# Attention and two gated layers in one kernel: four units normalized behind the value product, and a new order

## The chip, the cores and the metric

The kernel runs on one core of a Trainium2 chip. The metric is the device time of one execution in microseconds (us). The five engines are TensorE (PE; its weight loads are PEld), VectorE (DVE), ScalarE (ACT), GpSimd (POOL) and SyncE (SP), which issues the DMAs.

## The reference

Block-causal attention over 4 batches of 8 heads, 576 positions and 64 dimensions, then two feed-forward layers of 512 to 2048 to 512, in 32-bit floats.

```python
scores = scale * np.matmul(q, k.transpose(0, 1, 3, 2))
scores = np.where(mask, scores, -1000000000.0)     # mask: block of 64 of i >= that of j
scores = scores - np.max(scores, axis=-1, keepdims=True)
attn = np.exp(scores)
attn = attn / (np.sum(attn, axis=-1, keepdims=True) + 1e-09)
x = (attn @ v), heads side by side: 2304 tokens x 512
h = x @ w_in;  g = 1 where h >= 1, 0 where h <= -1, else (h + 1) ** 2 / 4;  x = g @ w_out
h = x @ w_in2; g = max(0.01 * h, h);                                       out = g @ w_out2
```

## The kernel before, in words

The attention is cut into 32 units: a pair of heads (the 128 partitions of a transposed result) and a part of the queries, "a" (the first 320 positions, three chunks of 64, 128 and 128 rows) or "b" (the last 256, two chunks). `unit_scores` multiplies queries by keys into PSUM slots of two banks (L586; L590 where the operands are split in two rounded parts) and calls `softmax`: per chunk a masked block is set (L482), the row maximum is taken on DVE (L484), ACT takes the exponential of every head and chunk into SBUF and sums its rows (L491), ACT adds 1e-9 (L495), DVE takes the reciprocal (L497), and POOL multiplies every probability by it (L502). Before that POOL clears the columns between the last key of a chunk and the next multiple of 128 (L606), and scales the queries (L547). `unit_values` transposes the probabilities in 128x128 blocks on PE (L680, against the identity), copies them out of PSUM on ACT or DVE (L685, L687), multiplies them by the values (L696), and evacuates the sum: for the first 256 tokens of the batch (the first four units, all of part "a") the rounded part to `XB[0]` on ACT (L707) and the rest on DVE (L708), the other columns through `xp` (L710) by DMA to DRAM (L711).

The weights of the first layer arrive as 64-bit words and are rebuilt in 16 steps (`w_float`) by ACT (L431, L442), POOL (L432, L445) and DVE (L434, L439, L445), two steps to a tile `W[p]`. `h1_block` then multiplies block i of 256 tokens by the eight tiles `W[p]`, 24 matmuls of 256 columns each into one PSUM bank (L756), which ACT and DVE evacuate (L762, L766, L767). Block 0 reads its tokens straight from `XB[0]`, all four quarters of it (one per pair of heads). The second product of the layer (L943) and both of the next (L1066, L1127) follow in a Strassen-like form with seven products.

No order is written by hand. Every operation is recorded with an engine, a cost and a priority, and `Plan.schedule` makes the order of each engine by a randomized list search with `TRIES` attempts from `SEED`; the chosen order is then issued as it is, so every engine works through its list in that order, and an instruction that waits holds up all behind it. PSUM has eight banks: slots 0, 1, 3 for attention, slot 2 as a fourth for the first seven units, and after these its two banks (4 and 5) for `h1_block`, of which block 0 uses only bank 4.

Of the kernel before, what the change touches and what calls it, by code (L numbers as in the profile page):

```python
# [25 lines left out]
SA = 320  # L26
# [23 lines left out]

AHEAD = 45.0


# [9 lines left out]

SEED, TRIES = 13, 42

# [239 lines left out]
def fused_kernel(ctx, tc, qk, qk2, v, w1, w2, out):  # L305
# [44 lines left out]
    def pool(cols, prio, fn, r, w, fixed=161):  # L350
        plan.op("POOL", fixed + 0.95 * cols, prio, fn, r, w, fixed != 200)

# [37 lines left out]
    def slot(i):  # L390

        return Bank(plan, (2 * i, 2 * i + 1), lambda: slots[i], {1: ps_b, 2: ps_c}.get(i, ps_a))

# [20 lines left out]
    def w_float(prio, fc):  # L414

        raw, sg = (C[8 + fc % 5].reg(z, m) for z, m in ((0, 1024), (1024, 512)))
        hs = XS.reg(turn("hs", (0, 512, 1024)), 512)
        src = w1[fc, :, 0:1024]  # L420
        t, j = W[fc // 2], fc % 2
        s = slice(512 * j, 512 * j + 512)

        def words():
            return raw.get().bitcast(I32).rearrange("p (n t) -> p n t", t=2)

        def upper():
# [11 lines left out]
        dve(512, prio, lambda: nc.vector.scalar_tensor_tensor(  # L439
            dst.get().bitcast(I32), hs.get().bitcast(I32), 3, sg.get().bitcast(I32),  # L440
            op0=ALU.logical_shift_left, op1=ALU.bitwise_or), [hs, sg], [dst])
        act(512, prio, lambda: nc.scalar.activation(t.get()[:, 0, s], dst.get(), AF.Copy), [dst], [(t, (j, j + 1))], sb=on_pool)  # L442

        def low():
            (nc.gpsimd if on_pool else nc.vector).tensor_tensor(t.get()[:, 1, s], dst.get(), bc(t.get()[:, 0, s]), op=ALU.subtract)  # L445
        rw = [dst, (t, (j, j + 1))], [(t, (2 + j, 3 + j))]
        if on_pool:
            plan.op("POOL", 1225, prio, low, *rw, True)
        else:
            dve(512, prio, low, *rw)  # L450

# [11 lines left out]
    dve(0, -100, lambda: nc.vector.memset(wz.get(), 0.0), [], [wz], fixed=200)  # L463
    zp = slot(2)
    for i in range(N_WARM):
        pe(427, -1000, lambda: nc.tensor.matmul(zp.get()[:, 0, 0:128], lhsT=wz.get(), rhs=wz.get(), start=True, stop=True), [wz], [zp])

# [3 lines left out]

    def softmax(prio, tag, s, parts):


        n = sum(len(p[2]) for p in parts)
        nm, sm, rs = small("nm", f"nm{tag}"), small("sm", f"sm{tag}"), small("rs", f"rs{tag}")
        i = 0
# [10 lines left out]
        for c, _, heads, view, probs, pbufs in parts:  # L488
            keys = CH[c][2]
            for k in range(len(heads)):  # L490
# [25 lines left out]
    def unit_scores(pair, part, prio, ring, room_):  # L516
# [16 lines left out]
        qk_room = qs, qo, nqk  # L533
        units[pair, part] = vt, pr, prob

# [64 lines left out]
        for c in ((0, 1, 2) if part == "a" else (3, 4)):  # L600
            keys = CH[c][2]
            a, b_ = PCOL[c] + keys, PCOL[c] + (keys + 127) // 128 * 128
            for hd in range(2):
                if a == b_:
                    continue
                pool(0, prio - 1, lambda a=a, b_=b_, hd=hd: nc.gpsimd.memset(prob(hd, a, b_), 0.0), [], [part_of(hd, a, b_)], fixed=200)  # L606

# [7 lines left out]
        for grp in groups:  # L615
            s = slot(ring[0])
            ring.append(ring.pop(0))

            def f(grp=grp, s=s):
                for i, (c, o) in enumerate(grp):  # L620
                    for hd in range(2):
                        score(s.get()[:, hd, o:o + CH[c][2]], c, hd, 0, CH[c][2], i == 0)
            pe(score_cost(sum(CH[c][2] for c, _ in grp)), prio, f, ready, [s])
            softmax(prio, f"{n}_{grp[0][0]}", s, [
                (c, o, (0, 1), lambda s=s, o=o, c=c: s.get()[:, :, o:o + CH[c][2]],
                 [probs(c, 0), probs(c, 1)], [pbuf(c, 0), pbuf(c, 1)]) for c, o in grp])
        if part == "b":
# [10 lines left out]
            for hd in range(2):  # L638
                if ss:
                    s = ss[hd]  # L640
                else:
                    s = slot(ring[0])

                    def f(hd=hd, s=s):
# [4 lines left out]
                    (4, 224, (hd,), lambda s=s: flat2(s)[:, 224:800].rearrange("p (h k) -> p h k", h=1),  # L649
                     [probs(4, hd)], [pbuf(4, hd)])])  # L650

# [10 lines left out]
    def unit_values(pair, part, prio, ring, evac):  # L662
        n = f"{part}{pair}"
        vt, pr, prob = units[pair, part]
        pts = []
        for i, blocks in enumerate(TILES[part]):
# [23 lines left out]
        ring.append(ring.pop(0))  # L690
        nq = SA if part == "a" else SB

        def f():
# [5 lines left out]
        pe(sum(x[3] for x in SUMS[part]) * 1.7 + 150, prio, f, [vt] + pts, [s])  # L699
        xp = P2.reg(turn("xp", (4032, 4352)), SA)  # L700
        b, kc = divmod(pair, NKC)
        c0 = b * S + (0 if part == "a" else SA)

        q0 = 256 if c0 == 0 else 0
        if q0:
            x = XB[0]
# [37 lines left out]
    def h1_block(i, p0, dp, hbanks):  # L744

        xt = XB[i]
        for p in range(NP2):
            pr = p0 + 2 * dp * p
            ps = bank(hbanks[0])
            hbanks.append(hbanks.pop(0))  # L750
            for j in range(2):
                fc = 2 * p + j
# [440 lines left out]
    for i in range(NBLK):  # L1193
# [108 lines left out]
```

## Time and profile before

| | |
|---|---|
| median of 3 runs | 947.88 us (946.68 to 949.87) |
| the profiled execution | 946.55 us |
| its span on the chip | 944.8 us |
| TensorE busy | 924.5 us, 98% of the span |
| DVE, ACT, POOL busy | 759.3, 537.9, 321.2 us |

How to read it: the span is from the first to the last instruction, and the execution is 1.75 us longer. Engines work side by side, each through its own list. "Busy" counts the time in which an engine works on an instruction; for TensorE that is close to a bound, since its matmuls follow each other without a gap wherever nothing is late. In a table by stretch, numbers in brackets count instructions (an fp32 matmul counts twice) and PEclk is the clock granted to TensorE as a share of 2.4 GHz. "A <- B" in a list of waits reads: A waited for B.

### The profile page before, as it was taken

To read this page: it belongs to the slowest core of one execution; us is meant where nothing else is said; L and a number is where in the kernel's file an instruction comes from. 1 tells how busy PE (TensorE), PEld (TensorE's weight loads), DVE (VectorE), ACT (ScalarE), POOL (GpSimd) and SP (SyncE) were. 2 spreads that over 40 slices of the span, in tenths; PEclk is the share of its full clock that TensorE was granted. 3 is DMA by queue.
4 is the path that set the end of the run, shared out by engine and by line. 5 is a ranking of instruction groups with operands and counts; after the bars stand their busy time and mean duration, and the time that the engine had idled before them with its cause. 6 is when DMAs were issued, how large, how long until landed. Compare 5 with 4: busy or idle time off the path is not lost.

```text
span 944.8 us, 19895 instructions
## 1 busy us (share of the span) xinstructions
PE 924.5 (98%) x7324; PEld 876.0 (93%) x7324; DVE 759.3 (80%) x1289; ACT 537.9 (57%) x1060; POOL 321.2 (34%) x626
## 2 busy tenths in 40 slices
PE   7799999999999999999999999999999999999998
PEld 5467888888889999999999999999999999999998
DVE  4988867877889765779979697678888899887967
ACT  5888777877879666663334343344535563333422
POOL 6997767677665831000000020236653000000000
PEclk8999999999999999999999999999999999999999
DMA  8767878895879789976434599978885983453433
GB/s 278 235 197 224 269 255 284 297 303 185 277 264 325 262 313 326 332 246 206 149 104 143 155 348 326 342 251 276 298 292 195 322 263 91 156 156 102 145 90 113
DMA packets 168130, 221.91 MB, mean 235 GB/s; under 512 B 10080, under 2 KB 141664, under 8 KB 168032
## 3 DMA queue, kind: packets, MB, share of 16 engines
q1 hardware_dynamic: 168032, 220.63, 72.0%
q8 instruction: 58, 0.95, 0.4%
q14 instruction: 40, 0.33, 0.1%
HBM read 139.85 MB, written 80.74 MB: 233 GB/s over the span
## 4 chain that ended last, share of the span: by engine, by line
PE 91%; DVE 3%; issue 1%; ACT 1%; DMA 1%; POOL 1%; SPq 0%; DVEq 0%; ACTq 0%
PE bank L1127 30%; PE bank L756 22%; PE bank L943 18%; PE bank L1066 6%; PE slot L680 5%; PE slot L696 5%; PE slot L586 2%; PE slot L590 2%; DMA w<-w 1%; ACT rp L491 1%; DVE ra L851 1%; POOL rp L502 1%; DVE ra L1086 0%; DVE rp L687 0%; DVE wraw L1115 0%
## 5 line engine op out<-in xcount | busy, mean ns | idle before, releaser
L756 PE MATMUL bank<-ra,w 128*128 128x256 f32 x1728 | 229.2, 286 | 1.0 <-DVE rg L767 1.0
L756 PEld LDWEIGHTS bank<-ra,w 128*128 128x128 f32 x1728 | 213.2, 189 | 10.1 <-issue 5.6
L943 PE MATMUL bank<-rp,w 128*128 128x288 f32 x1344 | 180.9, 296 | 0.2 <-DVE rp L883 0.2
L943 PEld LDWEIGHTS bank<-rp,w 128*128 128x128 f32 x1344 | 179.5, 189 | 0.9 <-DVE rp L883 0.4
L851 DVE TENSOR_TENSOR ra<-ra,bank 128x288 f32<-128x288 f32 (+2 forms) x280 | 126.3, 488 | 39.9 <-ACT ra L853 13.2
L1127 PE MATMUL bank<-w,rp 128*128 128x256 f32 x1014 | 148.6, 281 | 0.0
L1127 PEld LDWEIGHTS bank<-w,rp 128*128 128x128 f32 x1014 | 132.8, 188 | 0.0
L1112 ACT ACTIVATE rp<-ra 128x1024 fp32r<-128x1024 f32 (+1 forms) x48 | 47.3, 988 | 75.7 <-DVE ra L1086 71.4
L811 POOL TENSOR_TENSOR w<-w 128x128 f32<-128x128 f32 x128 | 65.6, 533 | 41.9 <-DVE w L807 40.5
L1127 PE MATMUL bank<-rp,w 128*128 128x256 f32 x508 | 76.8, 282 | 0.0
L947 ACT ACTIVATE ra<-ra 128x1152 f32<-128x1152 f32 x32 | 37.4, 1168 | 68.0 <-DVE ra L851 68.0
L767 DVE SCALAR_TENSOR_TENSOR rg<-bank,rg 128x512 f32<-128x512 f32 x72 | 49.3, 685 | 28.5 <-ACT rg L766 28.2
L1127 PEld LDWEIGHTS bank<-rp,w 128*128 128x128 f32 x508 | 67.5, 188 | 0.1
L762 ACT ACTIVATE rg<-bank 128x512 f32<-128x512 f32 x72 | 43.0, 598 | 33.0 <-PE bank L756 32.5
L878 POOL TENSOR_TENSOR xs<-xs,rp 128x576 f32<-128x576 f32 x1 | 1.5, 1500 | 175.3 <-DMA xs<-x2d 175.3
L1115 DVE TENSOR_TENSOR wraw<-ra,rp 128x1024 fp32r<-128x1024 f32 (+1 forms) x48 | 54.3, 1134 | 6.9 <-PE bank L1127 2.4
L1127 PE MATMUL bank<-w,wraw 128*128 128x256 f32 x294 | 58.7, 282 | 0.2 <-DVE wraw L1115 0.2
L1086 DVE TENSOR_TENSOR ra<-rp,ra 128x256 f32<-128x256 f32 (+2 forms) x102 | 44.4, 439 | 2.3
L1127 PE MATMUL bank<-rg,w 128*128 128x256 f32 x280 | 46.3, 282 | 0.0
L766 ACT ACTIVATE rg<-rg 128x512 f32<-128x512 f32 x72 | 45.5, 632 | 1.0
L1086 DVE TENSOR_TENSOR ra<-rp 128x512 f32<-128x512 f32 (+2 forms) x51 | 34.4, 676 | 14.5 <-DMA rp<-gd 13.5
L1127 PEld LDWEIGHTS bank<-w,wraw 128*128 128x128 f32 x294 | 45.0, 188 | 0.6 <-DVE wraw L1115 0.4
(170 smaller groups left out, 1840.4 us busy)
## 6 DMA issues: line engine op xcount, KB each, us to landing
rp<-gd SPq DMA_DIRECT2D x41, 512.0 KB, 4.2
wcd<-w SPq DMA_DIRECT2D x43, 448.0 KB, 5.2
gd<-ra SPq DMA_DIRECT2D x32, 576.0 KB, 4.6
gd<-rg SPq DMA_DIRECT2D x64, 256.0 KB, 4.0
w<-wcd SPq DMA_DIRECT2D x32, 512.0 KB, 6.8
w<-wcd SPq DMA_DIRECT2D x32, 384.0 KB, 6.2
w<-w SPq DMA_DIRECT2D x44, 256.0 KB, 5.2
w<-w SPq DMA_DIRECT2D x16, 512.0 KB, 4.7
```

The lines of the kernel that those rows point to most:

```text
L680: nc.tensor.transpose(s.get()[:, hd, o:o + 128], prob(hd, a, a + 128), ident.get())
L696: nc.tensor.matmul(s.get()[64 * hd:64 * hd + 64, 0, q0:q0 + m], lhsT=vt.get()[:, j, 64 * hd:64 * hd + 64], rhs=pts[i].get()[:, hd, o:o + m ...
L756: nc.tensor.matmul(ps.get()[:, 256 - j * 256:512 - j * 256], lhsT=win(fc, c, kc), rhs=xt[x].get()[:, kc], start=(k == 0 and kc == 0 and j ...
L767: dve(512, pv, lambda ps=ps, gt=gt: nc.vector.scalar_tensor_tensor(gt.get(), ps.get(), 1.0, gt.get(), op0=ALU.max, op1=ALU.min), [ps, gt], ...
L811: plan.op("POOL", 430, prio, lambda o=o, a=a, b=b, op=op: nc.gpsimd.tensor_tensor(sl(o), sl(a), sl(b), op=op), [(fx, (a, a + 1)), (fx, (b, ...
L851: dve(cols, prio, lambda: nc.vector.tensor_tensor(out(o), out(a), P[b][1](), op=op), [P[b][0], (slots, (a, a + 1))], [(slots, (o, o + 1))])
L943: nc.tensor.matmul(ps.get()[:, 0:HALF], lhsT=wc(1, p, cw, li, 128 * kc, 128 * kc + 128), rhs=r.get()[:, cx, kc], start=(k == 0 and kc == 0 ...
L1066: nc.tensor.matmul(ps[t].get()[:, 0:n], lhsT=wc(z, p, cw, li, 128 * t, 128 * t + 128), rhs=x.get()[:, n * zi:n * zi + n], start=(p == 0 an ...
L1086: dve(cols, pv, lambda f=f: nc.vector.tensor_tensor(*f(), op=ALU.subtract), r, [(tt, w)], port=True)
L1112: act(4 * n, pv, lambda tt=tt, ht=ht: nc.scalar.activation(s_(ht, 0, 4), s_(tt, 0, 4), AF.Copy), [tt], [ht], sb=True)
L1115: dve(4 * n, pv, lambda tt=tt, ht=ht, lt=lt: nc.vector.tensor_tensor(s_(lt, 0, 4), s_(tt, 0, 4), bc(s_(ht, 0, 4)), op=ALU.subtract), [tt, ...
L1127: nc.tensor.matmul(ps.get()[:, 256 * t:256 * t + w], lhsT=b if wide else g, rhs=g if wide else b, start=(p == 0 and k == 0 and t == 0), st ...
```

## The change

For the first four units (`LATE = 4`) POOL no longer multiplies the probabilities. The reciprocals of their row sums are kept in a small tile `late`, PE spreads them over 64 partitions per head by a product with the identity into the second bank of the slot that takes the values' product, ACT copies that to `xp`, DVE multiplies the values' product by it in `xp`, and the split for block 0 is made from `xp`. For the first two tiles of block 0 (`EARLY = 2`) the matmuls go quarter by quarter of the tokens, each needing one pair of heads alone. The columns between chunks are cleared only where the room last held the other part. Slot 2 is no longer lent to attention; both its banks serve `h1_block` from block 0 on. Some costs and the seed and number of attempts of the search differ, so that the order of all engines is new.

```diff
-SEED, TRIES = 13, 42
+SEED, TRIES = 15, 260
...
-    ps_c = psum("psr", "psr", "ps_c", (), ((2, True),), "right")
-    ps_e = psum("psr", "psr", "ps_e", ("psr",), ((2, False),), "right")
+    ps_e = psum("psr", "psr", "ps_e", (), ((2, False),), "right")
...
-        dve(8, prio, lambda: nc.vector.reciprocal(rs.get()[:, 0:n], rs.get()[:, 0:n]), [rs], [rs])
+        act(n, prio, lambda: nc.scalar.activation(r(), sm.get()[:, 0:n], AF.Copy, bias=1e-9), [sm], mine, sb=True, extra=60)
+        dve(8, prio, lambda: nc.vector.reciprocal(r(), r()), mine, mine)
+        if late is not None:
+            return
...
-                if a == b_:
+                if a == b_ or padded.get(room_) == part:
                     continue
...
+        if late is not None:
+            def f():
+                for i, c in enumerate((0, 1, 2) if part == "a" else (3, 4)):
...
+                        nc.tensor.matmul(s.get()[64 * hd:64 * hd + 64, 1, q:q + r], lhsT=late.get()[0:r, 2 * i + hd:2 * i + hd + 1].to_broadcast([r, 64]),
+                                         rhs=ident.get()[0:r, 0:r], start=True, stop=True, skip_group_check=True)
+            pe(nq * 1.7 + 150, prio, f, [ident, late], [s])
+            act(nq, prio, lambda: nc.scalar.activation(xp.get()[:, 0:nq], s.get()[:, 1, 0:nq], AF.Copy), [s], [xp])
...
+        if late is not None:
+            dve(nq, prio, lambda: nc.vector.tensor_tensor(xp.get()[:, 0:nq], s.get()[:, 0, 0:nq], xp.get()[:, 0:nq], op=ALU.mult), [s, xp], [xp])
+            if q0:
+                x = XB[0]
+                act(q0, prio, lambda: nc.scalar.activation(x[0].get()[:, kc], xp.get()[:, 0:q0], AF.Copy), [xp], [(x[0], (kc, kc + 1))], sb=True)
+                dve(q0, prio, lambda: nc.vector.tensor_tensor(
+                    x[1].get()[:, kc], xp.get()[:, 0:q0], bc(x[0].get()[:, kc]), op=ALU.subtract), [xp, (x[0], (kc, kc + 1))],
+                    [(x[1], (kc, kc + 1))], port=True)
...
+            for kc in range(NKC if i == 0 and p < EARLY else 0):
+                for j in range(2):
...
+                    pe(3 * 119.5, pr - 8 * (NKC - 1 - kc) + 0.01 * j, f, [(W[p], (j, j + 1)), (W[p], (2 + j, 3 + j))]
+                       + [(x, (kc, kc + 1)) for x in xt], [ps])
...
-    ring.append(2)
     attention(seq[:7])
-    ring.remove(2)
-    hb = [4]
+    hb = [4, 5]
```

Over the whole program PE gets 24 matmuls more (16 of 128 columns, 8 of 64), POOL 24 multiplications and 124 clears less (36 stay of 160), DVE four instructions more; ACT and SP keep their counts.

The order moves in three places that matter here. First, PE behind the warm-up matmuls (`rp` holds queries, keys and probabilities, `w_1` of L586 and L601 the third unit's queries; slots are named by `slot`). Before:

```order
L586 MATMUL slot_150<-rp_1_93 128x64 x2
L586 MATMUL slot_150<-rp_1_93 128x192 x2
L586 MATMUL slot_88<-rp_1_93 128x320 x2
L586 MATMUL slot_88<-w_1_110 128x64 x2
L586 MATMUL slot_88<-w_1_110 128x192 x2
L680 MATMUL slot_131<-ident,rp_1_93 128x128 x6
L680 MATMUL slot_132<-ident,rp_1_93 128x128 x6
L586 MATMUL slot_131<-w_1_110 128x320 x2
L696 MATMUL slot_150<-rp_1_90,rp_1_93 64x320 x2
L696 MATMUL slot_150<-rp_1_90,rp_1_93 64x256 x2
L696 MATMUL slot_150<-rp_1_90,rp_1_93 64x128 x2
```

Now (L601 is the old L586, L697 the old L680, L724 the old L696, L716 the spread):

```order
L601 MATMUL slot_149<-rp_1_96 128x64 x2
L601 MATMUL slot_149<-rp_1_96 128x192 x2
L601 MATMUL slot_134<-rp_1_96 128x320 x2
L697 MATMUL slot_135<-ident,rp_1_96 128x128 x6
L697 MATMUL slot_149<-ident,rp_1_96 128x128 x6
L601 MATMUL slot_135<-w_1_116 128x64 x2
L601 MATMUL slot_135<-w_1_116 128x192 x2
L716 MATMUL slot_134<-ident,latea_204 64x64 x2
L716 MATMUL slot_134<-ident,latea_204 64x128 x4
L601 MATMUL slot_149<-w_1_116 128x320 x2
L724 MATMUL slot_134<-rp_1_91,rp_1_96 64x320 x2
L724 MATMUL slot_134<-rp_1_91,rp_1_96 64x256 x2
```

The second chunk group of the second unit now takes the slot of the first unit's first group, and the transposes stand ahead of the third unit's scores; the spread of the first unit's reciprocals has come in ahead of its values.

Second, POOL at the same point of the program, where line 502 multiplies probabilities and L432 (now L433) rebuilds weights. Before:

```order
L432 TENSOR_SCALAR w_1_139<-w_1_139 128x512
L502 TENSOR_SCALAR rp_1_93<-rp_1_93,rsa_0_177 64x64 x2
L502 TENSOR_SCALAR rp_1_93<-rp_1_93,rsa_0_177 128x192
L502 TENSOR_SCALAR rp_1_93<-rp_1_93,rsa_2_186 128x320
L502 TENSOR_SCALAR rp_1_93<-rp_1_93,rsa_0_177 128x192
L502 TENSOR_SCALAR rp_1_93<-rp_1_93,rsa_2_186 128x320
L547 TENSOR_SCALAR rp_1_93<-rp_1_93 128x320
L502 TENSOR_SCALAR rp_1_90<-rp_1_90,rsa_2_221 128x320
L502 TENSOR_SCALAR rp_1_90<-rp_1_90,rsa_0_218 64x64
L502 TENSOR_SCALAR rp_1_90<-rp_1_90,rsa_0_218 128x192
L502 TENSOR_SCALAR rp_1_90<-rp_1_90,rsa_0_218 64x64
```

Now:

```order
L562 TENSOR_SCALAR w_1_116<-w_1_116 128x320
L433 TENSOR_SCALAR w_1_128<-w_1_128 128x512
L433 TENSOR_SCALAR w_1_156<-w_1_156 128x512
L562 TENSOR_SCALAR rp_1_96<-rp_1_96 128x320
L433 TENSOR_SCALAR w_1_180<-w_1_180 128x512
L562 TENSOR_SCALAR rp_1_96<-rp_1_96 128x256
L433 TENSOR_SCALAR w_1_219<-w_1_219 128x512
L446 TENSOR_TENSOR w_1_246<-w_1_156,w_1_246 128x512
L621 MEMSET rp_1_91 128x64
L433 TENSOR_SCALAR w_1_242<-w_1_242 128x512
```

The two units' twelve multiplications are gone (and twelve more behind them), and the rebuilding of weights has moved up into their place.

Third, PE where an "a" unit is transposed (L680, L697) and the next "a" unit's scores follow (L586, L601), with the matmuls of block 0 (L756; L793 in its first two tiles now, L803 in the others) between them. At the transposes of pair 5, before:

```order
L680 MATMUL slot_131<-ident,rp_1_93 128x128 x6
L756 MATMUL bank_638<-ra_1_288,w_1_417 128x256 x12
L586 MATMUL slot_131<-rp_1_93 128x64 x2
L586 MATMUL slot_131<-rp_1_93 128x192 x2
L680 MATMUL slot_132<-ident,rp_1_93 128x128 x6
L586 MATMUL slot_132<-rp_1_93 128x320 x2
L756 MATMUL bank_638<-ra_1_288,w_1_543 128x256 x4
```

Now, for the same pair:

```order
L697 MATMUL slot_149<-ident,rp_1_96 128x128 x6
L803 MATMUL bank_89<-ra_1_299,w_1_551 128x256 x12
L601 MATMUL slot_149<-rp_1_96 128x64 x2
L601 MATMUL slot_149<-rp_1_96 128x192 x2
L697 MATMUL slot_134<-ident,rp_1_96 128x128 x6
L803 MATMUL bank_89<-ra_1_299,w_1_551 128x256 x8
L803 MATMUL bank_88<-ra_1_299,w_1_682 128x256 x8
L601 MATMUL slot_134<-rp_1_96 128x320 x2
L724 MATMUL slot_135<-rp_1_91,rp_1_96 64x320 x2
```

And now, one such unit earlier, for pair 4:

```order
L697 MATMUL slot_149<-ident,rp_1_96 128x128 x6
L793 MATMUL bank_89<-ra_1_299,w_1_407 128x256 x3
L601 MATMUL slot_149<-rp_1_96 128x64 x2
L601 MATMUL slot_149<-rp_1_96 128x192 x2
L697 MATMUL slot_134<-ident,rp_1_96 128x128 x6
L601 MATMUL slot_134<-rp_1_96 128x320 x2
L724 MATMUL slot_135<-rp_1_91,rp_1_96 64x320 x2
```

In the second piece matmuls of block 0 stand between the transposes through a slot and the 128x320 scores that take this slot next; in the first, and now at pair 4, the scores stand right behind. Block 0 alternates between two banks. Its first matmuls now stand behind the second unit's values, in pieces of three to nine; before, they stood behind the fifth unit's.

## Rows read from the trace of the kernel before

**Rows 1.** The page, parts 1 and 2: busy time; granted clock in 40 slices.
```profile
PE 924.5 (98%) x7324; PEld 876.0 (93%) x7324; DVE 759.3 (80%) x1289; ACT 537.9 (57%) x1060; POOL 321.2 (34%) x626
...
PEclk8999999999999999999999999999999999999999
```

**Rows 2.** Stretch, its length; busy PE, PEld, DVE, ACT, POOL; clock, DMA share, GB/s.
```profile
0.00:24.00 24.00, 16.95 (x110) 12.80 (x112) 11.79 (x32) 14.06 (x53) 15.78 (x60) 0.86 0.80 274
24.00:60.00 36.00, 30.44 (x232) 19.82 (x228) 33.35 (x68) 30.70 (x98) 33.32 (x62) 1.00 0.71 226
60.00:110.00 50.00, 46.44 (x371) 37.62 (x372) 43.59 (x84) 41.91 (x119) 39.16 (x84) 1.00 0.78 233
110.00:900.00 790.00, 789.63 (x6276) 765.31 (x6275) 639.65 (x1044) 438.04 (x769) 232.99 (x422) 1.00 0.74 241
900.00:944.80 44.80, 41.06 (x342) 40.49 (x340) 30.94 (x64) 13.17 (x22) 0.00 (x0) 1.00 0.34 106
```

**Rows 3.** What TensorE waited for, whole span: us, times, longest.
```profile
PE slot L586 <- ACT rp L491: 6.2, 3, 5.3
PE slot L680 <- POOL rp L502: 2.2, 3, 1.0
PE slot L586 <- DVE rp L687: 2.2, 2, 1.1
PE slot L680 <- DVE ra L708: 1.3, 3, 0.7
...
PE bank L756 <- DVE rg L767: 1.0, 1, 1.0
PE slot L586 <- POOL w L811: 0.8, 1, 0.8
```

**Rows 4.** Stretches around the fall of the clock, columns as in Rows 2.
```profile
10.00:11.00 1.00, 0.00 (x0) 0.00 (x0) 0.00 (x0) 0.44 (x1) 0.40 (x1) 1.00 0.94 349
11.00:12.00 1.00, 0.00 (x0) 0.00 (x0) 0.71 (x2) 1.00 (x6) 0.91 (x2) 0.53 1.08 408
12.00:17.00 5.00, 4.25 (x20) 3.32 (x20) 2.55 (x8) 4.48 (x21) 4.67 (x10) 0.50 1.03 416
```

**Rows 5.** Line 502 alone until 33.5 us: length, busy POOL; clock, DMA share, GB/s.
```profile
0.00:33.50 33.50, 11.61 (x24) 0.90 0.81 271
```

**Rows 6.** Line 606 alone, until 110 us, same columns.
```profile
0.00:110.00 110.00, 8.71 (x84) 0.97 0.76 240
```

**Rows 7.** Timeline of TensorE: start, us, instructions, idle before.
```profile
12.71 1.44 PE L586 MATMUL slot<-w 64*128 64x64 f32 x8 [5.29 <-ACT rp L491]
14.08 3.18 PE L680 MATMUL slot<-ident,rp 128*128 128x128 f32 x12
...
18.25 1.41 PE L696 MATMUL slot<-rp,rp 128*64 128x320 f32 x12
```

**Rows 8.** ScalarE alone, three units' exponentials: length, busy ACT; clock, DMA.
```profile
7.09:21.13 14.04, 11.88 (x50) 0.76 0.97 350
```

**Rows 9.** Lines 434 and 708, until 110 us: ns min/median/max, first and last start.
```profile
L434 DVE SCALAR_TENSOR_TENSOR w<-w x16: 661/692/1284, 11.3 to 87.8; 128x512 int32<-128x512 int32 x16
...
L708 DVE TENSOR_TENSOR ra<-slot,ra x4: 416/424/425, 20.7 to 38.3; 128x256 fp32r<-128x256 f32 x4
```

**Rows 10.** Groups by shape until 110 us: busy us, mean ns.
```profile
L434 DVE SCALAR_TENSOR_TENSOR w<-w 128x512 int32<-128x512 int32 x16 | 13.1, 826 | 2.2 <-POOL w L432 2.2
...
L431 ACT ACTIVATE xs<-w 128x512 f32<-128x512 f32 x16 | 10.9, 681 | 1.8 <-DMA w<-w 0.8 <-DVE w L445 0.8 <-issue 0.2
...
L445 DVE TENSOR_TENSOR w<-xs,w 128x512 fp32r<-128x512 f32 x8 | 5.8, 730 | 0.0
...
L442 ACT ACTIVATE w<-xs 128x512 fp32r<-128x512 f32 x8 | 5.2, 645 | 0.0
...
L710 ACT ACTIVATE rp<-slot 128x320 f32<-128x320 f32 x4 | 1.8, 454 | 0.0
...
L710 ACT ACTIVATE rp<-slot 128x64 f32<-128x64 f32 x4 | 0.9, 231 | 0.0
```

More of the change, by code (lines that the diff above doesn't have):

```diff
@@ L51 @@
 AHEAD = 45.0
+LATE = 4
+EARLY = 2
 DELAY = {
@@ L390, in slot @@
     def slot(i):
[L392 removed]
+        return Bank(plan, (2 * i, 2 * i + 1), lambda: slots[i], {1: ps_b}.get(i, ps_a))
     def bank(i):
@@ L449, in w_float @@
         else:
-            dve(512, prio, low, *rw)
+            dve(512, prio, low, *rw, port=True)
     def win(fc, c, kc):
@@ L463, in fused_kernel, with softmax @@
     dve(0, -100, lambda: nc.vector.memset(wz.get(), 0.0), [], [wz], fixed=200)
-    zp = slot(2)
+    zp = bank(4)
     for i in range(N_WARM):
-        pe(427, -1000, lambda: nc.tensor.matmul(zp.get()[:, 0, 0:128], lhsT=wz.get(), rhs=wz.get(), start=True, stop=True), [wz], [zp])
+        pe(427, -1000, lambda: nc.tensor.matmul(zp.get()[:, 0:128], lhsT=wz.get(), rhs=wz.get(), start=True, stop=True), [wz], [zp])
     dummy = Buf(plan, "dummy", 1, lambda: const.tile([128, 8], F32, name="dummy"))
     act(8, -1000, lambda: nc.scalar.activation(dummy.get(), wz.get()[:, 0:8], AF.Exp), [wz], [dummy], extra=1280)
-    def softmax(prio, tag, s, parts):
+    def softmax(prio, tag, s, parts, late=None):
         n = sum(len(p[2]) for p in parts)
-        nm, sm, rs = small("nm", f"nm{tag}"), small("sm", f"sm{tag}"), small("rs", f"rs{tag}")
+        nm, sm = small("nm", f"nm{tag}"), small("sm", f"sm{tag}")
         i = 0
@@ L533, in unit_scores @@
         qk_room = qs, qo, nqk
-        units[pair, part] = vt, pr, prob
+        late = pt(st, [128, 6], F32, "late", f"late{n}", 6) if len(units) < LATE else None
+        units[pair, part] = vt, pr, prob, late
         q0, k0, nq, nk, nj = (SA, 0, SA, SA, 3) if part == "a" else (0, SB, SB, S, 5)
@@ L625, in unit_scores @@
                 (c, o, (0, 1), lambda s=s, o=o, c=c: s.get()[:, :, o:o + CH[c][2]],
-                 [probs(c, 0), probs(c, 1)], [pbuf(c, 0), pbuf(c, 1)]) for c, o in grp])
+                 [probs(c, 0), probs(c, 1)], [pbuf(c, 0), pbuf(c, 1)]) for c, o in grp], late)
         if part == "b":
@@ L663, in unit_values @@
         n = f"{part}{pair}"
-        vt, pr, prob = units[pair, part]
+        vt, pr, prob, late = units[pair, part]
         pts = []
@@ L691, in unit_values @@
         nq = SA if part == "a" else SB
+        xp = P2.reg(turn("xp", (4032, 4352)), SA)
+        if late is not None:
+            def f():
+                for i, c in enumerate((0, 1, 2) if part == "a" else (3, 4)):
+                    r = CH[c][1]
+                    q = CH[c][0] - (0 if part == "a" else SA)
+                    for hd in range(2):
+                        nc.tensor.matmul(s.get()[64 * hd:64 * hd + 64, 1, q:q + r], lhsT=late.get()[0:r, 2 * i + hd:2 * i + hd + 1].to_broadcast([r, 64]),
+                                         rhs=ident.get()[0:r, 0:r], start=True, stop=True, skip_group_check=True)
+            pe(nq * 1.7 + 150, prio, f, [ident, late], [s])
+            act(nq, prio, lambda: nc.scalar.activation(xp.get()[:, 0:nq], s.get()[:, 1, 0:nq], AF.Copy), [s], [xp])
         def f():
@@ L698, in f @@
                                      skip_group_check=True)
-        pe(sum(x[3] for x in SUMS[part]) * 1.7 + 150, prio, f, [vt] + pts, [s])
-        xp = P2.reg(turn("xp", (4032, 4352)), SA)
+        pe(sum(x[3] for x in SUMS[part]) * 1.7 + 230, prio, f, [vt] + pts, [s])
         b, kc = divmod(pair, NKC)
@@ L704, in unit_values @@
         q0 = 256 if c0 == 0 else 0
+        if late is not None:
+            dve(nq, prio, lambda: nc.vector.tensor_tensor(xp.get()[:, 0:nq], s.get()[:, 0, 0:nq], xp.get()[:, 0:nq], op=ALU.mult), [s, xp], [xp])
[5 more added lines that the diff above has]
+                    [(x[1], (kc, kc + 1))], port=True)
+            dma(128 * (nq - q0) * 4, prio, lambda: nc.sync.dma_start(x1d[:, kc, c0 + q0:c0 + nq], xp.get()[:, q0:nq]), [xp],
+                [(f"x1d{kc}", (c0 + q0, c0 + nq))])
+            return
         if q0:
@@ L750, in h1_block, with f @@
             hbanks.append(hbanks.pop(0))
-            for j in range(2):
+            for kc in range(NKC if i == 0 and p < EARLY else 0):
+                for j in range(2):
+                    def f(fc=2 * p + j, j=j, kc=kc, ps=ps):
+                        for k, (c, x) in enumerate(((0, 0), (1, 0), (0, 1))):
+                            nc.tensor.matmul(ps.get()[:, 256 - j * 256:512 - j * 256], lhsT=win(fc, c, kc),
+                                             rhs=xt[x].get()[:, kc], start=(k == 0 and kc == 0 and j == 0),
+                                             stop=(k == 2 and kc == NKC - 1), skip_group_check=True)
+                    pe(3 * 119.5, pr - 8 * (NKC - 1 - kc) + 0.01 * j, f, [(W[p], (j, j + 1)), (W[p], (2 + j, 3 + j))]
+                       + [(x, (kc, kc + 1)) for x in xt], [ps])
+            for j in range(0 if i == 0 and p < EARLY else 2):
                 fc = 2 * p + j
```

25 lines of the change are left out of this document (16 added, 9 removed).

## The prediction

> **What bounds the kernel now.** I read the page first. TensorE is busy for 924.5 of 944.8 us [rows 1], so the time is its work plus the 20 us in which it has none, and no other engine is near that share. The second row of the page shows the granted clock: 2.4 GHz everywhere but in the first slice.
>
> Then the table by stretch, to see where the 20 us lie [rows 2]. From 110 to 900 us TensorE lacks 0.37 us of 790. The last stretch lacks 3.7 us, the tail behind the last matmul (evacuation, sums, the output's DMA), which the change does not touch. All else is at the start: 7.05 us of the first 24, 5.56 of the next 36, 3.56 of the 50 after that. So the change can win only in the first 110 us, at most some 15 us of the 16.2 (TensorE cannot begin with the span), and anything that it adds to TensorE's work behind 110 us is paid in full. The same rows show what keeps TensorE waiting: from 24 to 60 us VectorE is busy for 33.35 of 36 us, POOL for 33.32, ScalarE for 30.70. Attention and the rebuilding of weights share these three.
>
> Then TensorE's waits [rows 3]: 5.3 us at once for exponentials (slots of the third unit's scores), 2.2 for POOL's multiplications in three pieces, 2.2 for VectorE's copies of transposes (L687) in two, 1.0 for the evacuation of block 0's only bank (L767), 0.8 for POOL's L811, and small ones.
>
> Last the stretch with the clock [rows 4, 7]: the 5.29 us gap ends at 12.71, and by 11 us the clock has fallen to 1.2 GHz, where it is until 17 us at least. TensorE's 4.25 busy us from 12 to 17 would be 2.1 at full rate.
>
> **The change, part by part.**
>
> *POOL.* The 24 multiplications of the first four units go: 11.61 us, all before 33.5 us [rows 5]. Of the clears 36 of 160 stay; 84 stood before 110 us with 8.71 us [rows 6], so at least 48 of these go, 5.0 us at 0.104 us each. Together 16.6 of POOL's 88.3 busy us before 110 us [rows 2]. POOL is not the path by itself; the gain is what waited for it.
>
> *The first three units.* The first transposes, twelve records at 14.08 us [rows 7], had POOL's multiplications before them, and now follow the exponentials. But ScalarE is in step with this stretch: it works from 7.09 us to the third unit's last sum at 21.1 us [rows 8] with some 2 us of breaks. Up to that point its new list has two rebuilding steps L431 less and one L442 more (-2 x 0.681 + 0.645), and the first spread's copy of 320 columns (0.454, by L710 of that shape) in place of the first unit's two evacuations, of 64 columns (0.231) and of 256 (between these two) [rows 10]. That is 0.7 to 0.95 us less; I take **-0.8 us**. The ends are 0 (the steps are only put off) and -2.9 us (the first unit's six multiplications, a quarter of the 11.61, were all that stood in TensorE's way). The two spreads and the three-slot ring of these units lie in the same stretch, beside ScalarE's work, and cost nothing as long as ScalarE sets it; without that cover they cost 1.2 us.
>
> *The gaps from 24 to 110 us*, 9.1 us [rows 2]. The 1.0 us for L767 goes, since block 0 has two banks. Of the 2.2 us for L687 one half stays: where pair 5 is transposed, and once more behind it, TensorE waited for the copy that frees the slot, and there matmuls of block 0 stand between now; but at pair 4 the scores stand right behind the transposes, and TensorE has to wait as it did. 1.1 us stays. Of the 2.2 us for POOL's multiplications the piece of the fourth unit goes and the others shrink, since POOL has a fifth less to do: 0.9 stays. The remaining 3.7 us are small waits for ScalarE, VectorE and POOL. Into that stretch the change puts 48 matmuls of block 0 in pieces of three to nine, that need one pair of heads each and not all four, from the second unit's values on, where before the first stood behind the fifth unit's. I let them fill half: 1.9 stays. So 3.9 us stay and **-5.2 us** go. The ends are -8.0 (all but the 1.1) and 0 (each piece itself waits for weights, which VectorE, POOL and ScalarE rebuild).
>
> *The spread on TensorE*: six fp32 matmuls for each unit, 320 columns for each of two heads that lie side by side in the array. The nearest row is the values' product of the same shape, 704 columns for each of two heads in 1.41 us at full clock [rows 7], so 320/704 of that, 0.64 us. If the heads did not overlap, 1.28. Two units lie in the first stretch; the other two are added work: **+1.3 us** (ends 0 and 5.1, all four unpaired and none covered).
>
> *VectorE*: per unit a product of 320 columns from PSUM (0.424 x 320/256 = 0.53) and a subtraction of 256 columns inside SBUF (0.37, half of the 0.730 of L445 for 512) in place of 0.424 [rows 9, 10]: 0.47, in four units 1.9 us more, on an engine that is 93% busy from 24 to 60 us. Against it stands that L434, with both inputs in SBUF, takes 661 ns at the least and 1284 at the most [rows 9], a slowing that I put down to POOL; its mean over 16 (0.826) is 134 ns above its median [rows 9, 10], and POOL has a fifth less to do. I give back 1.0 us over all such instructions, and count half of the rest as felt: **+0.4 us** (ends +1.9 and -0.6). *ScalarE*: the 320-column copies add about 0.9 us in four units, 0.2 of it behind the stretch counted above, beside other work.
>
> The Trainium skill, "SBUF — State Buffer", section "SBUF: two separate sides", speaks against the change here: VectorE and GpSimd share a port pair that is held by one of them for a whole instruction, and a VectorE instruction with two SBUF inputs is among those that take it. The old subtraction read PSUM and SBUF and never varied (416 to 425 ns [rows 9]), the new one reads SBUF twice. By the rule each of the four could stand behind a whole POOL instruction; at L434's worst, 0.62 us over its least, that is 2.5 us more and a sum 2.5 us higher, against the 0.4 us that the mean excess of L434 gives.
>
> *Left at nothing*: the new order behind 110 us. There TensorE waits for 0.37 us in 790 now, and VectorE is busy for 80% of it; if the search did worse, each lost microsecond would show. The warm-up on bank 4 and the later x1d writes hide beside TensorE.
>
> *Sum*: -0.8 - 5.2 + 1.3 + 0.4 = -4.3 us. The profiled execution took 946.55 us, 1.33 below the median; I set the change against the median: 947.88 - 4.3 = **943.6 us**.
>
> **The rivals.** About 0.3%, 2.8 us, is what a measurement can tell from no change, so "faster" is below 945.0 and "slower" above 950.7.
>
> *A, the forecast*, 943.6, with its own range 940 to 945.5.
>
> *B, the start empties.* The slots turn round so fast without POOL that the 5.29 us gap breaks into pieces, and the clock does not fall. For: every piece of the chain from exponential to transpose is then ScalarE's and TensorE's alone. Against: ScalarE is busy there anyway. Price: -8.0 in the gaps, -1.6 at the start, -2.1 for work no longer at half rate [rows 4], +1.3: -10.4, so 937.5 us. The Trainium skill, "TensorE: Matmul & The Clock Gate", section "Part 1: The HAM clock gate", says that idleness lowers the clock and activity lifts it; whether shorter gaps suffice to keep it, no row here shows.
>
> *C, VectorE is the pace.* From 24 to 110 us attention and weights need VectorE almost without a break, and the new pieces of block 0 need weights that VectorE makes. Then POOL's relief is worth nothing, only the 1.0 us of the second bank and the 0.8 us at the start are won, and 1.3 + 0.9 come on: +0.4, so 948.3 us. For: 93% busy. Against: TensorE's waits name POOL as often as VectorE [rows 3].
>
> *D, slower: the pieces of block 0 stand in the way.* TensorE takes its list in order, and the first piece stands right behind the second unit's values, ahead of the third unit's transposes. It needs the second rebuilt weight step, whose last part is on POOL behind the rebuilding of two further weights, which wait for their DMA. If that is late, attention stops with it. Price: all four spreads (2.6) and VectorE's 1.9 are felt, ScalarE's 0.9 too, and no gap goes: +5.4, so 953.3 us. It decides from the point where TensorE idles over 1 us ahead of the first piece. Against: POOL's new list has only weights and query scaling ahead of that part, none of the twelve multiplications that stood there.
>
> **How the numbers follow.** A 0.54, B 0.18, C 0.17, D 0.11. Range: the lower half of B and nearly all of D are left out, so 937 to 949. Faster: B and nearly all of A, 0.70. Same: C and A's upper end, 0.19. Slower: D, 0.11.
>
> **What would show it.** In the profile after: TensorE's busy time from 110 us on without new gaps, its gaps from 24 to 110 us at about 4 us; no wait for POOL's multiplication in the first four units; POOL's busy time before 110 us down by some 16 us; the spread at about 0.64 us for six matmuls; the new subtraction near 0.37 us; ScalarE's last sum of the third unit at about 20.3 us. The prediction is wrong if gaps of over 1 us stand ahead of the pieces of block 0, if VectorE is over 97% busy from 24 to 60 us, or if TensorE waits behind 110 us.

## The result and the profile after

The changed kernel takes 937.5 us (median of 4 runs, 936.0 to 939.6), the kernel before 947.3: a ratio of 0.989, with a 95% interval of 0.987 to 0.992. That is 9.8 us less, where the forecast was 4.3, at the lower edge of the range. The profiled execution after took 938.2 us, with a span of 936.4. The page's line of busy times, to set beside [rows 1]:

```profile
PE 922.3 (98%) x7372; PEld 870.9 (93%) x7372; DVE 758.3 (81%) x1293; ACT 538.1 (57%) x1060; POOL 301.6 (32%) x478
```

Stretches of the changed kernel, columns as in [rows 2]:

```profile
0.00:24.00 24.00, 20.39 (x144) 14.68 (x145) 15.50 (x37) 16.01 (x56) 11.56 (x41) 0.86 0.85 287
24.00:60.00 36.00, 32.70 (x260) 23.58 (x258) 31.55 (x66) 30.83 (x96) 25.56 (x37) 1.00 0.69 223
60.00:110.00 50.00, 48.64 (x392) 38.29 (x392) 42.23 (x83) 42.36 (x121) 33.40 (x54) 1.00 0.69 211
110.00:900.00 790.00, 788.23 (x6313) 762.70 (x6312) 642.68 (x1052) 437.94 (x770) 231.06 (x347) 1.00 0.75 244
900.00:936.40 36.40, 32.33 (x274) 31.61 (x272) 26.36 (x59) 10.94 (x20) 0.00 (x0) 0.99 0.30 95
```

TensorE's idle time in the first 24 us went from 7.05 to 3.61, in the next 36 from 5.56 to 3.30, in the 50 after that from 3.56 to 1.36. Behind 110 us 1.4 us of new gaps came in, and the tail lacks 4.07 instead of 3.74. All in all 14.1 us without work instead of 20.3, or 6.2 less; but the span is 8.4 less. So TensorE's busy time fell too, by 2.2 us, although the change gives it 24 matmuls more (48 records). That can't come from fewer instructions, and it is the larger riddle of this result.

What TensorE waited for now, where [rows 3] stood before (L601 is the old L586, L697 the old L680, L724 the old L696, L1174 the old L1127):

```profile
PE slot L601 <- ACT rp L492: 2.3, 1, 2.3
PE slot L601 <- DVE rp L704: 1.5, 1, 1.5
...
PE slot L697 <- ACT rp L492: 0.9, 3, 0.3
PE bank L1174 <- ACT rp L1159: 0.7, 1, 0.7
PE slot L724 <- DVE rsb L508: 0.7, 1, 0.7
PE slot L697 <- POOL rp L515: 0.6, 1, 0.6
```

The wait for L767 is gone, of the two for the copies of transposes one is left, POOL's multiplications hold it up once, and of the single wait of 5.3 us for exponentials 2.3 is the longest left. Small waits in the last product (L1174) have come in.

### The profile page after: what moved, and what is told of

It reads as the page before. It is cut to its first block, busy times and chain, and to the rows that moved or that the text cites. A ratio compares the mean times of both kernels' runs of the same rounds, so it can differ in the third digit from the quotient of the medians.

```text
span 936.4 us, 19910 instructions
## 1 busy us (share of the span) xinstructions
PE 922.3 (98%) x7372; PEld 870.9 (93%) x7372; DVE 758.3 (81%) x1293; ACT 538.1 (57%) x1060; POOL 301.6 (32%) x478
## 4 chain that ended last, share of the span: by engine, by line
PE 89%; DVE 4%; DMA 2%; ACT 2%; issue 1%; POOL 1%; SPq 0%; DVEq 0%; ACTq 0%; POOLq 0%
PE bank L1174 28%; PE bank L803 20%; PE bank L990 18%; PE bank L1113 6%; PE slot L697 5%; PE slot L724 5%; PE slot L601 3%; PE slot L605 2%; DMA w<-wcd 1%; ACT rp L492 1%; DVE ra L898 1%; PE bank L793 1%; DMA w<-w 1%; DMA gd<-ra 1%; DVE ra L1133 0%
## 5 line engine op out<-in xcount | busy, mean ns | idle before, releaser
L803 PE MATMUL bank<-ra,w 128*128 128x256 f32 x1680 | 224.9, 284 | 0.1
L803 PEld LDWEIGHTS bank<-ra,w 128*128 128x128 f32 x1680 | 206.7, 188 | 8.0 <-issue 6.4
L1174 PE MATMUL bank<-w,rp 128*128 128x256 f32 x1014 | 148.1, 280 | 0.9 <-ACT rp L1159 0.7
L1174 PEld LDWEIGHTS bank<-w,rp 128*128 128x128 f32 x1014 | 131.9, 189 | 1.9 <-ACT rp L1159 1.5
L1174 PE MATMUL bank<-rp,w 128*128 128x256 f32 x508 | 78.5, 279 | 0.0
L858 POOL TENSOR_TENSOR w<-w 128x128 f32<-128x128 f32 x128 | 68.9, 562 | 16.7 <-DVE w L854 14.9
L814 DVE SCALAR_TENSOR_TENSOR rg<-bank,rg 128x512 f32<-128x512 f32 x72 | 49.4, 686 | 24.5 <-ACT rg L813 23.8
L1174 PEld LDWEIGHTS bank<-rp,w 128*128 128x128 f32 x508 | 68.0, 188 | 0.0
L1174 PE MATMUL bank<-w,wraw 128*128 128x256 f32 x294 | 56.6, 279 | 0.0
L1174 PE MATMUL bank<-rg,w 128*128 128x256 f32 x280 | 48.6, 280 | 0.4 <-ACT rg L1159 0.4
L1174 PEld LDWEIGHTS bank<-w,wraw 128*128 128x128 f32 x294 | 44.3, 189 | 0.0
L1133 DVE TENSOR_TENSOR ra<-rp,ra 128x256 f32<-128x256 f32 (+2 forms) x102 | 41.9, 417 | 2.3 <-DMA x2d<-ra 0.2
L1113 PE MATMUL bank<-rp,w 128*128 128x384 f32 x224 | 43.6, 336 | 0.0
```

The lines of the kernel that those rows point to most:

```text
L803: nc.tensor.matmul(ps.get()[:, 256 - j * 256:512 - j * 256], lhsT=win(fc, c, kc), rhs=xt[x].get()[:, kc], start=(k == 0 and kc == 0 and j ...
L814: dve(512, pv, lambda ps=ps, gt=gt: nc.vector.scalar_tensor_tensor(gt.get(), ps.get(), 1.0, gt.get(), op0=ALU.max, op1=ALU.min), [ps, gt], ...
L858: plan.op("POOL", 430, prio, lambda o=o, a=a, b=b, op=op: nc.gpsimd.tensor_tensor(sl(o), sl(a), sl(b), op=op), [(fx, (a, a + 1)), (fx, (b, ...
L1113: nc.tensor.matmul(ps[t].get()[:, 0:n], lhsT=wc(z, p, cw, li, 128 * t, 128 * t + 128), rhs=x.get()[:, n * zi:n * zi + n], start=(p == 0 an ...
L1174: nc.tensor.matmul(ps.get()[:, 256 * t:256 * t + w], lhsT=b if wide else g, rhs=g if wide else b, start=(p == 0 and k == 0 and t == 0), st ...
```

## Experiments

Two questions were open: which part of the change shortened the start, and why TensorE's work takes less time.

The second has a suspect that no row before showed. The `late` tiles lie in SBUF ahead of the large work tiles (`rm`: the operands `ra`, `rg`, `rp`, `xs`, `wraw`, `wsg`) and push these 192 bytes up in every partition, away from the weights' tiles (`wp`), which stay. The first pair of kernels moves the tiles and touches nothing else.

**The move alone, on the kernel before.**

```diff
+    st.tile([128, 48], F32, tag="pad", name="pad", bufs=1)
     slots = {}
```

> The kernel before with one unused tile of 192 bytes per partition ahead of the work tiles, so that these lie where they lie after the change; no instruction and no order differs. Theory 1 (the spacing of matmuls depends on where the work tiles lie, and the four small tiles of the change moved them): the median step from matmul to matmul from 460 to 575 us falls from 119.8 to about 119.0 ns, TensorE's busy time by 4 to 6 us, and the time to 941 to 944 us. Theory 2 (the spacing belongs to the order, or differs from execution to execution): the time stays at 946 to 949 us.

Measured: 936.3 us against 947.7, ratio 0.989 (0.987 to 0.990). An unused tile brings all that the whole change brought, and more than I expected of it. The trace of the kernel before (all of 110 to 900 us, then a piece of L1127 in which all but a handful of the records are matmuls of 256 columns), columns: stretch, its length, TensorE's busy time and records, clock, DMA share, GB/s:

```profile
110.00:900.00 790.00, 789.63 (x6276) 1.00 0.74 241
460.00:540.00 80.00, 80.00 (x674) 1.00 0.48 145
```

The same with the move by 192 bytes, in the slowest of its five executions (941.0 us; the others took 934.7 to 937.8):

```profile
110.00:900.00 790.00, 788.48 (x6324) 1.00 0.74 243
460.00:540.00 80.00, 79.95 (x678) 1.00 0.49 147
```

Same instructions, same order, same clock: 48 records more get done between 110 and 900 us. At 790 us / 6276 = 0.126 us each that is 6.0 us, and this execution was 5.6 us faster than that of before.

**The change without the move.** The reciprocals are kept in the operand of the warm-up matmuls, which is free by then.

```diff
-        late = pt(st, [128, 6], F32, "late", f"late{n}", 6) if len(units) < LATE else None
+        k = len(units)
+        late = Buf(plan, (id(st), "late"), 6, lambda: wz.get()[:, 6 * k:6 * k + 6]) if k < LATE else None
```

> The changed kernel with the four tiles of reciprocals kept inside the warm-up operand, so that the work tiles lie where they lay before; instructions and order are those of the changed kernel. Theory 1 (place of the work tiles): 941 to 944 us, 4 to 6 us above the changed kernel. Theory 2 (order, or the execution): 936 to 940 us as the changed kernel.

Measured: 944.5 us, ratio 0.9963 (0.9951 to 0.9975) to before. Order and instructions are those of the changed kernel, so what the change does on purpose is worth 3.2 us in the old place (2.4 to 4.6 by the interval), and the move makes up the rest. Its stretches:

```profile
0.00:24.00 24.00, 19.10 (x148) 1.00 0.88 296
24.00:60.00 36.00, 32.94 (x258) 1.00 0.68 223
60.00:110.00 50.00, 48.63 (x395) 1.00 0.69 208
110.00:900.00 790.00, 789.30 (x6267) 1.00 0.75 243
```

The idle time of the first 110 us is 4.90 + 3.06 + 1.37 = 9.3 us, against 16.2 before and 8.3 after: the gaps are closed here as well. What differs from the changed kernel behind the start is the records done from 110 to 900 us, 6267 against 6313; ahead of it the clock, 1.00 in the first 24 us against 0.86.

**How far a move counts.** The same unused tile with 64 and with 128 bytes, and one of 192 bytes in the first pool instead, which moves weights and work tiles together:

```diff
+    st.tile([128, 16], F32, tag="pad", name="pad", bufs=1)     # b_shift64; [128, 32] in b_shift128
...
+    const.tile([128, 48], F32, tag="pad", name="pad", bufs=1)  # b_both192
```

> The kernel before with the work tiles moved by 64 bytes instead of 192. If what counts is the place within 128 bytes, 64 does what 192 did (192 = 128 + 64): 934 to 941 us, steps of 117 to 119 ns from 460 to 575 us. If it is a place within a longer stretch (256 or 512 bytes), the time may lie anywhere between 935 and 948 us, and if only the very move by 192 matters, it stays at 946 to 949.

> The kernel before with the work tiles moved by 128 bytes. If the place within 128 bytes counts, nothing changes: 946 to 949 us, with the steps of 115, 120 and 122 ns of the kernel before. If any move helps, 934 to 941.

> The kernel before with the weights' tiles and the work tiles moved by 192 bytes together, so that their distance is that of before and only the place of both is new. If the place of the operands against each other counts, 946 to 949 us as before. If the place of the work tiles by itself counts, 934 to 941 us, as with the work tiles alone moved.

Measured: 64 bytes 936.4 us (ratio 0.988, 0.987 to 0.990); 128 bytes 950.4 (1.0044, 1.0028 to 1.0060); both together 946.7 (1.0000, 0.9991 to 1.0009). The move by 128, which I expected to change nothing, costs 3.7 us. The two stretches of each, first with 64 bytes:

```profile
110.00:900.00 790.00, 788.61 (x6377) 1.00 0.74 243
460.00:540.00 80.00, 79.95 (x703) 1.00 0.51 154
```

With 128 bytes:

```profile
110.00:900.00 790.00, 789.70 (x6254) 1.00 0.74 242
460.00:540.00 80.00, 80.00 (x663) 1.00 0.46 137
```

With both moved by 192:

```profile
110.00:900.00 790.00, 788.74 (x6274) 1.00 0.74 242
460.00:540.00 80.00, 80.00 (x673) 1.00 0.47 143
```

In the piece from 460 to 540 us one matmul comes every 80 us / 674 = 118.7 ns before, every 113.8 with 64 bytes, 120.7 with 128, 118.0 with 192, and 118.9 with both moved. So it is not the place of the work tiles that counts, since with both moved they lie where 192 bytes alone put them: it is their place relative to the weights', or the places of both at once.

**Other places, with the changed kernel.** Moves of 64, 224 and 288 bytes in all against the kernel before; the changed kernel has 192.

```diff
+    st.tile([128, 16], F32, tag="pad", name="pad", bufs=1)     # a_only64, with late in the warm-up operand
+    st.tile([128, 8], F32, tag="pad", name="pad", bufs=1)      # a_plus32, beside the late tiles
+    st.tile([128, 24], F32, tag="pad", name="pad", bufs=1)     # a_plus96, beside the late tiles
```

> The changed kernel, its four small tiles kept inside the warm-up operand, the work tiles moved by 64 bytes alone. By the theory that the place within 128 bytes counts it is the changed kernel again: 934 to 938 us, with steps of 113, 117 and 118 ns. If the move by 64 is better than that by 192, as the single fastest run so far (932.99 us, the kernel before moved by 64) may suggest, 930 to 934.

> The changed kernel with the work tiles moved by 32 bytes more (224 against the kernel before, 96 within 128). If what counts is in which half of 128 bytes a row begins, relative to the weights, this place lies across the two halves and the time is between: 937 to 944 us, with a mixture of steps. If 64-byte units are read whole, a start at 96 or at 64 does the same: 934 to 938.

> The changed kernel with the work tiles moved by 96 bytes more (288 against the kernel before, 32 within 128). As the run before, from the other side: between 937 and 944 us if a start across the halves costs a part, 943 to 946 if it counts as the old place.

> The changed kernel once more, beside the kernels above on one chip. Everything the change does on purpose is worth 3.2 us by the pair with the work tiles in their old place. If it is worth as much with them in the new one, this is 3 us under the kernel before with the move alone (936.3), so 933 us; if the move has made TensorE the lesser bound at the start and the gain is lost in the spread from execution to execution, 935 to 940 us.

Measured, each against the kernel before: a_only64 935.0 us (0.986, 0.984 to 0.989), a_again 935.9 (0.988, 0.987 to 0.990), a_plus32 946.5 (0.999, 0.998 to 1.001), a_plus96 944.5 (0.997, 0.996 to 0.999). a_plus32 came out above the old place (944.5 for the change there), where I had it between. Over all places tried, relative to the weights:

| move of the work tiles, bytes | kernel before | changed kernel |
|---|---|---|
| 0 | 947.3 | 944.5 |
| 64 | 936.4 | 935.0 |
| 128 | 950.4 | not run |
| 192 | 936.3 | 937.5, 935.9 |
| 224 | not run | 946.5 |
| 288 | not run | 944.5 |

64 and 192 are fast, all others slow. An odd number of 64-byte units is the pattern that fits these six places; 224 and 288, half a unit off, do not get a part of it.

In the fast places the change on purpose can hardly be seen: 935.0 to 937.5 against 936.3 and 936.4. Against the kernel before the intervals overlap (0.984 to 0.989 for the change at 64, 0.987 to 0.990 for the move by 64 alone). The sum of both would have been 933 us, and it didn't come. The gaps are not back; the kernel before moved by 64 idles in its first 110 us as it did:

```profile
0.00:24.00 24.00, 16.93 (x106) 0.86 0.80 274
24.00:60.00 36.00, 30.83 (x236) 1.00 0.71 223
60.00:110.00 50.00, 45.76 (x368) 1.00 0.79 234
```

7.07 + 5.17 + 4.24 = 16.5 us of idle time, against 8.4 in the changed kernel with the same move (a_only64). But from 110 to 900 us that execution did 6377 records, a_only64's 6350, and in the piece from 460 to 540 us 703 against 697:

```profile
110.00:900.00 790.00, 787.96 (x6350) 1.00 0.75 245
460.00:540.00 80.00, 80.00 (x697) 1.00 0.50 150
```

27 records are 3.4 us, as much as the change was worth in the old place. It is one trace of each, so whether the new order costs this or the execution did stays open.

In that piece two paces occur, near 114 and near 118 ns, and they go with the place, in both kernels: 703 and 697 records with a move by 64 bytes, 678 to 681 in the four traces with 192 (b_shift, a_nolate, and the changed kernel twice):

```profile
460.00:540.00 80.00, 80.00 (x681) 1.00 0.48 140
```

In the last layer the product swaps its operands (`lhsT=b if wide else g, rhs=g if wide else b`): there the weights move through TensorE and the work tiles are held in it, and 192 bytes are ahead. From 800 to 920 us there are 1013 records in the kernel before, 1020 in both kernels with 64, and 1022 to 1030 in the four traces with 192; here b_shift64, then a_again:

```profile
800.00:920.00 120.00, 120.00 (x1020) 1.00 0.44 128
...
800.00:920.00 120.00, 119.91 (x1030) 1.00 0.45 136
```

So which operand moves seems to matter beside the distance, and no single piece ranks the places: with 288 bytes, a slow place, the first has 683 records and the second 1003. Executions of one kernel can lie 5 us apart as well (933.0 to 938.0 for b_shift64, while 17 of the kernel before beside it lay between 946.1 and 948.2).

**The longer search alone.**

```diff
-SEED, TRIES = 13, 42
+SEED, TRIES = 15, 260
```

> The kernel before with the seed and the number of attempts of the changed kernel, nothing else. If the longer search alone brings the gain, TensorE's idle time in the first 110 us falls from 16.2 to about 10 us and the time to 938 to 942 us. If the gain needs the work that the change takes off POOL and the pieces of block 0, the idle time stays at 14 us or more and the time at 944 to 948 us. I expect the second.

Measured: 953.4 us, ratio 1.0062 (1.0049 to 1.0075). It is slower, which I had not expected. The first stretches:

```profile
0.00:24.00 24.00, 16.10 (x86) 0.79 0.73 255
24.00:60.00 36.00, 28.37 (x190) 0.92 0.67 208
60.00:110.00 50.00, 47.13 (x378) 0.99 0.71 220
```

and two of its waits:

```profile
PE slot L586 <- POOL rp L502: 6.1, 1, 6.1
PE slot L586 <- ACT rp L685: 3.8, 3, 2.4
```

18.4 us are idle in the first 110 us, 6.1 of them in one wait for POOL's multiplications; that is 2.2 more than before. Over the whole span TensorE is idle for 23.8 us, 3.5 more, and busy for 2.4 more, with its clock at 0.79 and 0.92 in the first two stretches. So the new seed brings nothing by itself, and an order drawn anew can cost 6 us.

**The change with the old seed**, in the old place (beside this edit, that of a_noshift).

```diff
-SEED, TRIES = 15, 260
+SEED, TRIES = 13, 42
```

> The changed kernel with the work tiles in their old place, searched from the seed and with the attempts of the kernel before (13 and 42), to see how much of the 3.2 us hangs on the order that the search happened to find. If the change's own parts bring them, 943 to 946 us and TensorE idle for under 11 us of the first 110; if the order brings them, 947 us or more.

Measured: 943.9 us, ratio 0.9962 (0.9948 to 0.9975). Another order, the same gain:

```profile
0.00:24.00 24.00, 20.23 (x140) 0.86 0.79 261
24.00:60.00 36.00, 34.44 (x280) 1.00 0.76 261
60.00:110.00 50.00, 47.45 (x383) 1.00 0.67 194
110.00:900.00 790.00, 788.50 (x6265) 1.00 0.75 243
```

3.77 + 1.56 + 2.55 = 7.9 us idle. Two orders of the change stand at 0.9963 and 0.9962 (3.2 and 2.9 us), so these 3 us are more likely owed to its parts than to one search; two draws are few, with 6 us between two draws of the kernel before.

**POOL's multiplications back**, in the place of the change.

```diff
-LATE = 4
+LATE = 0
...
+    st.tile([128, 48], F32, tag="pad", name="pad", bufs=1)
```

> The changed kernel with POOL's multiplications back in all units (LATE = 0) and a tile of 192 bytes that keeps the work tiles in place; the order is searched anew. If taking the multiplications off POOL is what shortens the start, TensorE waits for the multiplications ahead of the first units' transposes again, its idle time in the first 24 us rises from 3.6 to 6 us or more, and the time is 939 to 943 us, the four spreads (3.4 us of TensorE) saved against it. If they were hidden, the time is 934 to 937 us, since those 3.4 us of matmuls go.

Measured: 939.0 us (936.3 to 944.3), ratio 0.991 (0.989 to 0.993).

```profile
0.00:24.00 24.00, 18.89 (x108) 0.86 0.80 271
24.00:60.00 36.00, 31.24 (x239) 1.00 0.65 206
60.00:110.00 50.00, 46.28 (x376) 1.00 0.72 217
```

```profile
PE slot L698 <- POOL rp L516: 2.0, 3, 0.7
```

13.6 us idle in the first 110 us, 5.3 more than in the changed kernel, 2.0 of it for POOL's multiplications; 5.1 of them lie in the first 24 us, where I expected 6 or more. Against that stand the four spreads. The time is 1.5 to 3 us above the changed kernel's, less than the scatter of this kernel: the sign is likely, the size open. EARLY, the second bank and the fewer clears were not taken out one by one, since every such kernel is searched anew, and the search alone moved one by 6 us.

## Why the prediction was right, and where it wasn't

The sum held for what it summed. It gave 4.3 us less; the change in the old place takes 944.5 us with the one order and 943.9 with the other, 3.2 and 2.9 less than the kernel before beside it. The step that failed is "*Left at nothing*: the new order behind 110 us" and, beneath it, that TensorE's work there takes the time it took: it did not wait less there, its matmuls came closer together. The order itself was rightly left at nothing, since in the old place 6267 records were done from 110 to 900 us with the new one and 6276 with the old. I read the four tiles as a place for reciprocals and not as 192 bytes that move every operand behind them, and I took busy time for close to a bound, where the kernel before, moved by 64 bytes, is busy for 911.5 us and not 924.5 with the same list.

That the range held the result is luck: its lower end reached to rival B, which gave 937.5 us by another mechanism. Of that one part came, the 5.29 us gap is broken up; the clock, which was to stay up and bring 2.1 us, fell as before. One term of B's price, the 1.6 us at the start, comes from no row besides. The changed kernel, columns as in [rows 4]:

```profile
11.00:12.00 1.00, 1.00 (x5) 1.00 (x6) 0.95 (x3) 0.64 (x3) 0.50 (x1) 0.50 1.08 411
12.00:17.00 5.00, 5.00 (x29) 2.79 (x29) 4.13 (x13) 4.14 (x15) 2.32 (x5) 0.50 1.03 414
```

By its own steps:

*The gaps from 24 to 110 us.* Forecast 3.9 us left of 9.1; 3.30 + 1.36 = 4.7 are left. The second bank took away the wait for L767, matmuls of block 0 covered two places of copies, and the wait that was expected at pair 4 came (columns as in [rows 7]):

```profile
13.75 1.53 PE L716 MATMUL slot<-ident,latea 64*64 64x64 f32 x12
...
19.93 0.92 PE L716 MATMUL slot<-ident,latea 64*64 64x64 f32 x12
...
23.46 0.98 PE L793 MATMUL bank<-ra,w 128*128 128x256 f32 x6
...
26.90 0.92 PE L716 MATMUL slot<-ident,latea 64*64 64x64 f32 x12
...
54.03 0.81 PE L601 MATMUL slot<-rp 64*128 64x320 f32 x4 [1.54 <-DVE rp L704]
```

The scores at 54.03 us waited 1.54 us for the copy of the transposes in their slot; I had taken 1.1. The first piece of block 0, at 23.46 us, waited for nothing, so rival D fell.

*The first units.* ScalarE's last sum of the third unit was to come at about 20.3 us:

```profile
19.52 0.20 ACT L492 ACTIVATION_READ_ACCUMULATOR w<-slot,nma 128x1 f32 x1
```

It ends at 19.72, 1.4 us earlier than before where 0.8 was taken. TensorE lost 3.4 us of idle time in the first 24 us, but 2.5 of it were filled by the two spreads.

*POOL.* 15.78 + 33.32 + 39.16 = 88.3 us busy before 110 us, now 11.56 + 25.56 + 33.40 = 70.5; 17.8 less where 16.6 was forecast.

*The spread* was the term that was mis-sized. Groups by shape in the first 110 us, columns as in [rows 10]:

```profile
L716 PE MATMUL slot<-ident,latea 128*64 128x128 f32 x32 | 3.1, 322 | 0.0
...
L733 DVE TENSOR_TENSOR rp<-slot,rp 128x320 f32<-128x320 f32 x4 | 2.0, 490 | 0.7 <-ACT rsa L507 0.6
L737 DVE TENSOR_TENSOR ra<-rp,ra 128x256 fp32r<-128x256 f32 x4 | 1.9, 478 | 0.0
...
L716 PE MATMUL slot<-ident,latea 64*64 64x64 f32 x16 | 1.5, 266 | 0.1
```

Its six matmuls are twelve records and take 0.92 us at full clock (at 19.93 and 26.90 us), and 1.53 at 1.2 GHz (at 13.75); forecast 0.64, with 1.28 as the bound for heads that do not overlap. The sum had two spreads on the path, 1.3 us. The two behind the first stretch, at 26.90 and 36.45 us, take 0.85 us each until the next matmul starts (at 27.75 and 37.30), 1.7 together.

*VectorE.* The product from PSUM took 0.490 us (forecast 0.53), the subtraction 0.478 (0.37):

```profile
L737 DVE TENSOR_TENSOR ra<-rp,ra x4: 399/419/674, 22.1 to 44.1; 128x256 fp32r<-128x256 f32 x4
```

Three of the four subtractions are near 0.41 us, one took 0.674. The Trainium skill's rule in "SBUF — State Buffer", section "SBUF: two separate sides", spoke of whole POOL instructions that such an instruction can stand behind. The one at 22.05 us started while POOL's L433 ran (21.24 to 22.45 us) and took 0.26 us more than the others; two others ran wholly inside multiplications of POOL (L515, 1.33 and 1.01 us long) and took 0.40 and 0.41. So the rule agrees with one of the four, and the price by the mean was the better one. VectorE from 24 to 60 us was busy for 31.55 us of 36, less than before: rival C fell as well.

*Behind 110 us* 1.4 us of new gaps came; none was forecast, and TensorE waiting there was one of the prediction's own signs of being wrong. They need no new order: there TensorE lacks 0.4 us in the kernel before, 1.5 and 1.4 with the work tiles moved by 192 and by 64, 1.3 with both moved, and 0.7 in the changed kernel in the old place.

## What to carry to other kernels

A new small tile moves every tile behind it, and here a move by 64 bytes was worth three times what the change did on purpose: before a change is credited with a gain, run the old kernel with an unused tile of the same size, and the new one without the move. Where TensorE is the bound, look at the matmuls done in a fixed, long stretch of the program that the edit did not touch; if that number differs, the cause need not be in the instructions that were edited. And where a search makes the order, draw a second order before believing a few microseconds.

## What the runs showed of the hardware that I had not expected

The pace of matmuls of 256 columns with a stationary operand of 128x128 depends on where their two operands lie against each other in a partition of SBUF: 118.7 ns and 120.7 at moves of 0 and 128 bytes, 113.8 and 114.8 in two executions at 64, 118.0 and 117.5 at 192; between 110 and 900 us 6254 to 6377 records from one and the same list. Both moved together gave 118.9. The Trainium skill, "SBUF — State Buffer", section "SBUF: two separate sides", says that TensorE's port waits on no other engine; that may well hold here, since the relation is between TensorE's own two operands, but what it is inside the engine no run shows. Which of the work tiles has to lie where was not tried either.

With the same list of instructions the clock of the first 24 us fell in some executions and not in others: granted clock 0.86 in the changed kernel, 1.00 in a_noshift, where TensorE was busy for 20.39 and 19.10 us of them. The longest wait there was 2.3 us in both.
